# Loading the rows of the first two loop blocks at the end of attention, in a fused attention and mixture-of-experts kernel

## The chip, the cores and the metric

The kernel runs on one core of one Trainium2 chip. The metric is the device time of one execution in microseconds. The median of three runs of the kernel before is 657.54 us (655.55 to 658.39).

A core has five engines that run side by side and wait for one another by semaphores: TensorE (PE in the profile; PEld is its loading of weights), VectorE (DVE), ScalarE (ACT), GpSimd (POOL) and SyncE (SP), which here issues most of the DMAs. Each takes its own instructions in program order, so an instruction that waits holds up all that are queued behind it on its engine.

## The reference

Attention with keys and values averaged over groups of 8 rows, then a mixture of 8 experts in which each token goes to the one expert with the highest logit:

```python
k_p, v_p = (x.reshape(B, H, Sp, 8, D).mean(axis=3) for x in (k, v))
attn = softmax(q @ k_p.T / sqrt(D))
x = (attn @ v_p).transpose(0, 2, 1, 3).reshape(4608, 512)
expert_idx = argmax(x @ w_gate)                   # 8 experts
y = maximum(x[of e] @ w1[e], 0) @ w2[e]           # w1: 512x1024, w2: 1024x512
out = gate_w[:, None] * y                         # gate_w: softmax weight of the chosen expert
```

B = 8 batches, H = 8 heads, S = 576 rows, D = 64. The inputs are drawn with a fixed seed.

## The kernel before

**Attention** runs as 36 units of 128 tokens (line 912). A unit's tokens get their logits, and groups of four units (at the end, of two) are routed by `route(gidx)`: VectorE finds each token's expert, TensorE counts ranks, and GpSimd scatters each token's row, with its number and its gate, into `xs`, a table in HBM in which every expert has its own segment. `cum` holds the running counts; `c16` is its copy for TensorE. Small steps of this routing are kept in a list (`later`) and put in between the attention's own instructions (`fill`, `drain`), and scatters go through a list of their own (`flush`). Hooks (`put(unit, place, function)`) set other work at places in the units: loads, and splits of weights.

All products of the experts are made of 16-bit halves: a 32-bit number is split into a high half (ScalarE) and the rest (VectorE), and three matmuls replace one. This holds for weights (`wsplit`) and for rows (`split_x`).

**A block** is up to 256 rows of one expert. `up(s, f, n)` makes 128 of the 1024 hidden columns, with 12 matmuls; `relu_hi` (ScalarE) and `relu_lo` (VectorE) split the result; `finish(s, j, half)` makes the output for 128 of the rows from half of the hidden columns, with 12 matmuls. Both need the rows with the columns on the partitions: `turn` or `trans` transposes the halves of the rows by DMA from SyncE, and after `trans`, which goes by way of `xTs`, `arrive` (VectorE) copies them into `xT`.

**Block 0** is the first 256 rows of expert 0. When 256 tokens of expert 0 have been counted early enough, `early_load` (unit 29) brings its rows into `xg`, GpSimd splits them, `turn` transposes them, and the first three `up` run in units 33 to 35. Then `okf` is 1 and the table starts at block 1.

**The hand-over** (lines 972 to 1173): the other five `up` of block 0 run while VectorE ends the routing (`counted`, `ordered`, `ended`) and works out a table (`table`, 29 small steps) of which rows each loop block takes and which experts' weights come next. `tables` transposes it on TensorE into `tabs`. Only then come block 0's four `finish`, and the loads of blocks t=0 and t=1, whose places are read from `tabs`. Their rows are split, t=0's are transposed, the next expert's weights are loaded whole (`wwhole`, two DMAs of 2 MB), then t=2's rows are loaded, and t=1's rows are transposed.

**The loop** (line 1208) takes one block a turn. In turn t SyncE transposes the rows of t+2 and loads those of t+3, and in turns where an expert begins (and in t=0) ScalarE and VectorE split the next expert's weights (`part`) behind the split of rows:

```python
        arrive()
        split_x()
        part(s, en)
        if full:
            for half in range(2):
                finish(s, 1, half)
        take(1)
```

`take` reads the outputs from PSUM, `give` scatters them from GpSimd; `keep_ids`, `move_ids` and `take_ids` pass rows' numbers and gates along on GpSimd and mark `xg` as free. PSUM tiles named `pq` share two buffers, taken in turn.

Of the kernel before, what the change touches and what calls it, by code (L numbers as in the profile page):

```python
# [11 lines left out]
I32 = mybir.dt.int32  # L12
# [19 lines left out]
def kernel(  # L32
# [147 lines left out]
    for x in range(2):  # L180
# [17 lines left out]
    oki = consts.tile([1, 1], I32, name="oki")  # L198
    gC, gA, gB = (consts.tile([128, 2], F32, name=n) for n in ("gC", "gA", "gB"))
# [22 lines left out]
    xg, xg2 = (VB[i].rearrange("p y c s x -> p (y c s x)").bitcast(F32)[:, 0:2 * XW]  # L222
               .rearrange("p (j x) -> p j x", j=2) for i in (2, 0))
# [361 lines left out]
    EARLY = len(bounds) - 4  # L585

    def route(gidx):
# [39 lines left out]
        def rank():  # L627
            oh = Z["oh"][:, 0:gs]
            pm = psA.tile([128, 512], F32, name="pq", bufs=2)
            pr = pm[:, 0:gs * E].rearrange("p (u e) -> p u e", e=E)  # L630
            nc.tensor.matmul(pr, before, oh, start=True, stop=False, skip_group_check=True)
            nc.tensor.matmul(pr, ones, Z["c16"][:, None, :].to_broadcast([128, gs, E]), start=False, stop=False,
                             skip_group_check=True)
            for u in range(1, gs):
                nc.tensor.matmul(pr[:, u:gs, :], ones, oh[:, 0:gs - u, :], start=False, stop=False,
                                 skip_group_check=True)
            Z["pr"] = pr

# [48 lines left out]

        if gidx == len(bounds) - 1:
            return [top, away, best, lowest, before_all, onehot, count, carry], rank, \
                [ranked, spot, spot_int, total, ident_ids, guard, gate], soft, scatters  # L690
        chain = [top, away, best, lowest, before_all, onehot, soft, rank, count, ranked, carry, total, spot, spot_int,
                 ident_ids, guard, gate, scatters]
        if gidx == EARLY - 1:
            chain += [before_all, early_pe, early_int, early_shift, lambda: (flush(), KVS.update(early=1))]
        for f in chain:
            later(gidx, f, f in (rank, early_pe))
# [161 lines left out]

    put(28, "sp", blank_x, xg)
# [9 lines left out]
    put(31, "sp", turn)  # L869

# [134 lines left out]

    def sent(st):
        for o in scat + soon:
            tc.declare_no_dep(st.ins, o.ins, reason="rows of other tokens")
        scat.append(st)
        return st  # L1010
# [17 lines left out]
    def ended():  # L1028
        pe = psA.tile([128, 512], F32, name="pq", bufs=2)
        pq["nb"] = pe[:, 0:E]  # L1030
        nc.tensor.matmul(pq["nb"], ones, pq["lt"], start=True, stop=True)
        for f in back:
            f()
        scatters()
        flush()
        pad_rest()
        table()

    def table():
        nb, pos, more = pq["nb"], pq["pos"], pq["more"]  # L1040
        tcl, ex_, sb, blk, nw = (tf[:, NK + j:NK + j + 1] for j in range(5))
        g = work.tile([128, 2, E], F32, name="gg")
        end = work.tile([128, E], F32, name="end")
        n3 = work.tile([128, 3], F32, name="n3")
        sel = work.tile([128, 4, E], F32, name="sel", bufs=1)
        exk, got, par = (work.tile([128, n], F32, name=m) for n, m in ((4, "exk"), (4, "got"), (4, "par")))
        tot = work.tile([128, 1], F32, name="tot")
# [3 lines left out]
        V.tensor_reduce(tot, end, axis=AX.X, op=OP.max)  # L1051
        V.tensor_scalar(tcl, tot, -1.0, tv, op0=OP.add, op1=OP.min)
# [29 lines left out]
    def tables():  # L1082
        pt = psA.tile([128, 512], F32, name="pq", bufs=2)
        nc.tensor.transpose(pt[0:NK, 0:128], tf[:, 0:NK], ident)
        V.tensor_copy(tabs, pt[0:NK, 0:NT])

    for f in range(FC):
        if f >= len(UPAT):
            up(0, f, BLK)
        if f + 1 == 5:  # L1090
            counted()
            ordered()
        if f + 1 == 6:
            ended()
        if f + 1 == 8:
            tables()
        if f in (1, 3):
            relu_hi(f // 2)
    for k in (2, 3):
        relu_hi(k)  # L1100
    for k in range(4):
        relu_lo(k)
    views = [x.rearrange("p a b c -> p (a b c)") for x in qt] + [x.rearrange("p c x -> p (c x)")[:, 0:2048] for x in kv[1:]]
    views = [x.bitcast(F16) for x in views]
    W1[1] = [x.rearrange("p (c f) -> p c f", c=DC) for x in views[:2]]
    W2[1] = [x.rearrange("p (c f) -> p c f", c=FC) for x in views[2:]]
    pY.append(psA.tile([128, 512], F32, name="pq", bufs=2))
    pH[3] = psA.tile([128, 512], F32, name="pq", bufs=2)
    for j, half in ((1, 0), (1, 1), (0, 0), (0, 1)):
        finish(0, j, half)  # L1110
# [22 lines left out]
    xh2 = kv[1].rearrange("p c x -> p (c x)")[:, 0:1024].bitcast(F16).rearrange("p (j a x) -> p j a x", j=2, a=2)  # L1133
    blank_x(xg2)
    load_x(0)
    load_x(1, xg2)
    for j in range(2):
        x, h = xg[:, j, 0:Dm], xh[:, j]
        nc.scalar.activation(h[:, 0], x, AF.Copy)
        V.tensor_tensor(h[:, 1], x, h[:, 0], op=OP.subtract)  # L1140
    keep_ids()
    move_ids()
    turn()

    def at_place(j):
        return nc.values_load(tab[0:1, 1 + j:2 + j], engines=[ENG.SP], min_val=0, max_val=E - 1)

    wwhole(at_place(1), 0)
    load_x(2)
    split_x(xg2, xh2)  # L1150
    keep_ids(xg2)
    trans(xh2)
# [105 lines left out]
```

## Time and profile before

| | |
|---|---|
| median of three runs | 657.54 us (655.55 to 658.39) |
| the profiled execution's own time | 649.4 us |
| its span, first to last instruction | 647.3 us |
| mean granted clock of TensorE | 0.962 |
| TensorE busy | 584.5 us (90%) |
| VectorE, ScalarE, GpSimd busy | 349.6, 289.1, 258.2 us |

The span is the time from the first to the last instruction of the profiled execution, 2.1 us below the time of that execution. Times in the timeline are microseconds from the start of the span. A busy TensorE is not one at its peak, as matmuls overlap in the pipeline. The loop's first `up` starts at 240.78, and the loop takes the rest of the span.

### The profile page before, as it was taken

The page shows a single profiled execution, that of the slowest core. Times are in us where ns is not written, and L with a number is a line of the kernel's source. Part 1 is how long each engine was busy: PE and PEld are TensorE (multiplying, and loading weights), DVE is VectorE, ACT ScalarE, POOL GpSimd, SP SyncE. Part 2 cuts the span into 40 slices and gives each one's busy share as a digit, 9 for nine tenths or more (in the row PEclk, how much of TensorE's full clock was granted, in tenths as well). Part 3 has the DMA queues.
Part 4 walks back from the last instruction along what each step waited for, and adds up shares of the span by engine and source line. Part 5 has one row for each costly group of instructions (what it writes and reads, how often), then busy time and mean ns, then how long its engine had stood idle before and what let it go on. Part 6 is the DMA issues. An engine that isn't in the chain of part 4 may idle for free. (4 is left out here: it accounts for less than half of the span.)

```text
span 647.3 us, 15827 instructions
## 1 busy us (share of the span) xinstructions
PE 584.5 (90%) x4630; PEld 430.7 (67%) x4631; DVE 349.6 (54%) x767; ACT 289.1 (45%) x634; POOL 258.2 (40%) x475
## 2 busy tenths in 40 slices
PE   6669979878878779899999999999999999999985
PEld 4558878778867537566776677676667677667653
DVE  5669969899898821712362221237122641273783
ACT  1447858658864121621452222236223622263772
POOL 5793576887466621330232012223113032214134
PEclk9979989779999988999999999999999999999988
DMA  8971797957734459497377213335723392329200
GB/s 252 320 226 56 226 311 177 294 157 239 200 107 102 171 144 338 118 379 218 99 225 229 54 39 85 97 79 164 250 59 94 68 327 75 92 43 331 41 30 10
DMA packets 104170, 105.59 MB, mean 163 GB/s; under 512 B 62278, under 2 KB 72518, under 8 KB 104136
## 3 DMA queue, kind: packets, MB, share of 16 engines
q1 hardware_dynamic: 97496, 85.46, 46.9%
q0 software_dynamic: 6640, 19.71, 8.4%
q8 instruction: 18, 0.29, 0.2%
q14 instruction: 16, 0.13, 0.1%
HBM read 71.77 MB, written 22.06 MB: 145 GB/s over the span
## 5 line engine op out<-in xcount | busy, mean ns | idle before, releaser
L964 PEld LDWEIGHTS <-bd 128*128 128x128 f16 x936 | 91.8, 98 | 106.9 <-issue 2.1
L958 DVE SCALAR_TENSOR_TENSOR bd<-ps,bd 128x512 f16<-128x512 f32 x44 | 30.1, 690 | 154.2 <-ACT bd L954 154.1
L1167 POOL TENSOR_TENSOR spacer<-ql,iG 1x1 f32<-1x1 f32 x44 | 22.7, 516 | 188.3 <-ACT ql L1163 187.3
L495 ACT ACTIVATE both<-ps,nmx 128x72 f32<-128x72 f32 x288 | 68.7, 326 | 34.1 <-DVE nmx L488 33.5
L478 PE MATMUL ps<-bd,qT 128*128 128x144 f32 x256 | 50.4, 326 | 11.0 <-ACT both L495 5.8
L964 PE MATMUL po<-kv,bd 128*128 128x512 f16 x264 | 58.8, 379 | 0.0
L964 PE MATMUL po<-w,bd 128*128 128x512 f16 x264 | 58.8, 379 | 0.0
L954 ACT ACTIVATE bd<-ps 128x512 f16<-128x512 f32 x44 | 26.1, 596 | 72.9 <-PE L900 58.3
L1168 POOL DMA_INDIRECT out_dram<-ql,iG x44 | 44.7, 1017 | 21.2 <-issue 20.1
L318 POOL TENSOR_TENSOR st<-kv 128x1280 f32<-128x1280 f32 x14 | 40.8, 2913 | 25.8 <-DMA kv<-in_k_dram 23.3
L660 POOL DMA_INDIRECT x_by_expert<-both,rpos x36 | 35.2, 979 | 37.6 <-DVE ri L566 16.1
L902 PE MATMUL ps<-kv,qt 128*128 128x256 f16 (+1 forms) x176 | 46.7, 270 | 2.7 <-DVE qt L113 2.6
L900 PE MATMUL ps<-kv,w 128*128 128x256 f16 (+1 forms) x176 | 44.3, 265 | 5.1 <-DMA kv<-bd 3.4
L478 PEld LDWEIGHTS ps<-bd,qT 128*128 128x128 f32 x256 | 40.1, 215 | 12.8 <-ACT both L495 9.7
L964 PE MATMUL pq<-kv,bd 128*128 128x512 f16 x216 | 48.1, 379 | 0.0
L901 PE MATMUL ps<-kv,qt 128*128 128x256 f16 (+1 forms) x176 | 46.8, 270 | 0.0
L900 PE MATMUL ps<-kv,qt 128*128 128x256 f16 (+1 forms) x176 | 46.7, 270 | 0.1
L902 PE MATMUL ps<-kv,w 128*128 128x256 f16 (+1 forms) x176 | 44.3, 265 | 0.7 <-DVE qt L113 0.6
L964 PE MATMUL pq<-w,bd 128*128 128x512 f16 x192 | 44.4, 389 | 0.0
L901 PE MATMUL ps<-kv,w 128*128 128x256 f16 (+1 forms) x176 | 44.3, 265 | 0.0
L900 PEld LDWEIGHTS <-w 128*128 128x128 f16 x352 | 34.8, 99 | 10.2 <-issue 3.9
L902 PEld LDWEIGHTS <-qt 128*128 128x128 f16 x352 | 35.2, 100 | 7.2 <-issue 3.7
(246 smaller groups left out, 1364.8 us busy)
## 6 DMA issues: line engine op xcount, KB each, us to landing
st<-in_moe_w_dram SPq DMA_DIRECT2D x8, 2048.0 KB, 13.4
both<-in_moe_w_dram SPq DMA_DIRECT2D x6, 2048.0 KB, 12.9
vb<-x_by_expert SPq DMA_DIRECT2D x17, 514.0 KB
kv<-in_k_dram SPq DMA_DIRECT2D x7, 1024.0 KB
kv<-in_v_dram SPq DMA_DIRECT2D x7, 1024.0 KB
qt<-in_q_dram SPq DMA_DIRECT2D x6, 1024.0 KB
st<-in_moe_w_dram SPq DMA_DIRECT2D x4, 1024.0 KB
qt<-in_q_dram SPq DMA_DIRECT2D x4, 512.0 KB
```

The costliest lines, as they stand in the source:

```text
L318: nc.gpsimd.tensor_tensor(t1, src[:, :, 0:4 * D], src[:, :, 4 * D:], op=OP.add)
L478: nc.tensor.matmul(ps[:, x * 2 * KP:(x + 1) * 2 * KP], t[:, h, :], BD[b % 3][:, :, h, :], start=True, stop=True)
L495: nc.scalar.activation(p[:, h * KP:(h + 1) * KP], ps[:, x * KP:(x + 1) * KP], AF.Exp, bias=nmx[:, x:x + 1], scale=-1.0)
L660: st = nc.gpsimd.indirect_dma_start(out=xs, out_offset=bass.IndirectOffsetOnAxis(ap=Z["pos"][:, u:u + 1], axis=0), in_=X[:, u, :], in_offs ...
L900: nc.tensor.matmul(dst, wh, xT[:, d, 0:n], start=(d == 0), stop=False)
L901: nc.tensor.matmul(dst, wh, xT[:, DC + d, 0:n], start=False, stop=False)
L902: nc.tensor.matmul(dst, wl, xT[:, d, 0:n], start=False, stop=(d == DC - 1))
L954: nc.scalar.activation(hT[0][:, 2 * k:2 * k + 2, :].rearrange("p f t -> p (f t)"), pH[k], AF.Relu)
L958: V.scalar_tensor_tensor(l, pH[k], 0.0, h, op0=OP.max, op1=OP.subtract)
L964: nc.tensor.matmul(y, hT[x][:, f, 128 * j:128 * j + 128], W2[s][z][:, f, :], start=(half == x == z == f == 0), stop=(half == z == 1 and f ...
L1167: nc.gpsimd.tensor_tensor(spacer[:, 0:1], ys[j][0:1, 0:1], iG[0:1, j:j + 1].bitcast(F32), op=OP.add)
L1168: st = nc.gpsimd.indirect_dma_start(out=out, out_offset=bass.IndirectOffsetOnAxis(ap=iG[:, j:j + 1], axis=0), in_=ys[j], in_offset=None, b ...
```

## The change

- A flag `okf2` is set when, with group 7 (units 28 to 31) about to be counted, expert 0 already has 768 tokens and block 0 was loaded early.
- If it is set, `load_again` in unit 35 loads the rows of blocks 1 and 2 of expert 0, which are then t=0 and t=1. It needs the scatters of groups 0 to 6. `xg2` moves from a buffer that attention uses to its end to one that is free by then, and its blanking (`blank_x`) to unit 32.
- The rows of t=0 are split and transposed while block 0's `up` run, those of t=1 are split behind the table. If the flag is not set, both are loaded and split behind the table as before.
- t=0's rows go by `trans` and `arrive` and no longer by `turn`. The transposition of t=1's rows comes ahead of the weights' load.
- The steps of the hand-over are put in another order: `counted` and `ordered` one `up` later, `ended` as well; `relu_lo` of the first half ahead of `ended`; the table's work behind `relu_lo`; and `tables` behind three of the four `finish`.

```diff
+    xh2 = kv[1].rearrange("p c x -> p (c x)")[:, 0:1024].bitcast(F16).rearrange("p (j a x) -> p j a x", j=2, a=2)
...
+    AGAIN = EARLY + 1
...
+            if gidx == AGAIN:
+                nc.tensor.matmul(pm[:, 256:257], ones, Z["c16"][:, 0:1], start=True, stop=True, skip_group_check=True)
+                Z["pa"] = pm[:, 256:257]
...
+        def again():
+            V.tensor_scalar(okf2, Z["pa"], 768.0, okf, op0=OP.is_ge, op1=OP.mult)
+
+        def again_int():
+            V.tensor_copy(oki2, okf2[0:1, :])
...
+        if gidx == AGAIN:
+            x = chain.index(ranked) + 1
+            chain[x:x] = [again, again_int, lambda: (flush(99, AGAIN - 1), KVS.update(again=1))]
...
+    def load_again():
+        assert KVS.pop("again")
+        ok = nc.values_load(oki2[0:1, 0:1], engines=[ENG.SP], min_val=0, max_val=1)
+        with tc.If(ok > 0):
+            lds = [nc.sync.dma_start(x, xs[b * BLK:b * BLK + BLK, :].rearrange("(j p) x -> p j x", p=128))
+                   for b, x in ((1, xg), (2, xg2))]
+        for ld in lds:
+            for o in scat[bounds[AGAIN][0]:]:
+                tc.declare_no_dep(ld.ins, o.ins, reason="rows of other tokens")
+            soon.append(ld)
+
+    put(32, "q", blank_x, xg2)
...
+    put(35, "sp", load_again)
...
-        table()
+        ends()
...
-        if f + 1 == 5:
+        if f + 1 == 6:
             counted()
             ordered()
-        if f + 1 == 6:
+            split_x()
+            trans()
+            relu_lo(0)
+            relu_lo(1)
+        if f + 1 == 7:
             ended()
-        if f + 1 == 8:
-            tables()
         if f in (1, 3):
             relu_hi(f // 2)
     for k in (2, 3):
         relu_hi(k)
-    for k in range(4):
+    for k in (2, 3):
         relu_lo(k)
+    table()
+    split_x(xg2, xh2)
...
+    pt = psA.tile([128, 512], F32, name="pq", bufs=2)
     pY.append(psA.tile([128, 512], F32, name="pq", bufs=2))
+    finish(0, 0, 0)
+    finish(0, 1, 0)
+    finish(0, 1, 1)
+    tables(pt)
     pH[3] = psA.tile([128, 512], F32, name="pq", bufs=2)
-    for j, half in ((1, 0), (1, 1), (0, 0), (0, 1)):
-        finish(0, j, half)
+    finish(0, 0, 1)
...
-    blank_x(xg2)
-    load_x(0)
-    load_x(1, xg2)
-    for j in range(2):
-        x, h = xg[:, j, 0:Dm], xh[:, j]
-        nc.scalar.activation(h[:, 0], x, AF.Copy)
-        V.tensor_tensor(h[:, 1], x, h[:, 0], op=OP.subtract)
+    ok = nc.values_load(oki2[0:1, 0:1], engines=[ENG.SP, ENG.Activation, ENG.DVE], min_val=0, max_val=1)
+    with tc.If(ok < 1):
+        load_x(0)
+        load_x(1, xg2)
+        split_x()
+        trans()
+        split_x(xg2, xh2)
+    arrive()
     keep_ids()
     move_ids()
-    turn()
...
+    keep_ids(xg2)
+    trans(xh2)
     wwhole(at_place(1), 0)
     load_x(2)
-    split_x(xg2, xh2)
-    keep_ids(xg2)
-    trans(xh2)
```

`ends` is the first four lines of the old `table`, up to the total of blocks.

## Rows read from the trace of the kernel before

**Rows 1.** Timeline of TensorE, first `up` of blocks t=2 and t=3: start, us, instruction.
```profile
288.00 0.27 PE L900 MATMUL ps<-kv,w 128*128 128x256 f16 x1
...
308.84 0.27 PE L900 MATMUL ps<-kv,qt 128*128 128x256 f16 x1
```

**Rows 2.** Timeline of TensorE, hand-over and t=0; in brackets idle time before, and releaser.
```profile
217.15 0.17 PE L984 MATMUL pq<-c,ones 128*128 128x8 f16 x1 [0.84 <-DVE c L977]
...
225.06 0.27 PE L1084 MATMUL pq<-ident,tf 128*8 128x128 f32 x1 [3.70 <-DVE tab L1080]
...
240.78 0.37 PE L900 MATMUL ps<-kv,w 128*128 128x256 f16 x1 [3.40 <-DMA kv<-bd]
...
259.08 5.34 PE L964 MATMUL po<-w,bd 128*128 128x512 f16 x24
...
266.11 0.27 PE L900 MATMUL ps<-kv,w 128*128 128x256 f16 x1 [1.69 <-ACT qt L111]
```

**Rows 3.** 1 us stretches: PE, PEld, DVE, ACT, POOL busy; PEclk, DMA, GB/s.
```profile
245.00:246.00 1.00, 1.00 (x6) 0.73 (x5) 0.00 (x0) 0.00 (x0) 0.54 (x4) 0.50 1.03 303
...
255.00:256.00 1.00, 1.00 (x6) 0.47 (x5) 0.66 (x1) 0.00 (x0) 0.00 (x0) 1.00 1.08 363
256.00:257.00 1.00, 1.00 (x7) 0.47 (x5) 0.00 (x0) 0.00 (x0) 0.00 (x0) 1.00 2.13 107
```

**Rows 4.** Timeline of VectorE in block t=0.
```profile
259.47 0.69 DVE L847 COPY kv<-kv 128x2048 f16<-128x2048 f16 x1 [3.81 <-DMA kv<-kv]
...
262.53 1.22 DVE L836 TENSOR_TENSOR bd<-vb,bd 128x1024 f16<-128x1024 f32 x1 [2.36 <-ACT bd L835]
263.67 4.62 DVE L113 SCALAR_TENSOR_TENSOR qt<-st,qt 128x1024 f16<-128x1024 f32 x4
```

**Rows 5.** Timeline of GpSimd, hand-over and t=0.
```profile
205.40 0.97 POOL L660 DMA_INDIRECT x_by_expert<-both,rpos  x1 [0.22 <-issue]
...
226.96 0.98 POOL L226 MEMSET vb<- 128x1028 f32 x1
...
234.73 0.19 POOL L815 TENSOR_TENSOR gC<-vb,zf 128x2 f32<-128x2 f32 x1 [6.63 <-DMA vb<-x_by_expert]
...
259.75 0.47 POOL L815 TENSOR_TENSOR gC<-vb,zf 128x2 f32<-128x2 f32 x1 [14.20 <-SPq L1208]
```

**Rows 6.** Timeline of the SyncE queue, hand-over and t=0.
```profile
230.78 2.76 SPq L1122 DMA_DIRECT2D vb<-x_by_expert  x2
...
236.17 2.64 SPq L840 DMA_TRANSPOSE kv<-bd  x2
240.09 0.96 SPq L86 DMA_DIRECT2D st<-in_moe_w_dram  x2
...
246.18 11.28 SPq L843 DMA_TRANSPOSE kv<-kv  x1
263.92 1.98 SPq L843 DMA_TRANSPOSE kv<-bd  x1
```

**Rows 7.** Costliest groups of the page: weight loads of `finish`.
```profile
L964 PEld LDWEIGHTS <-bd 128*128 128x128 f16 x936 | 91.8, 98 | 106.9 <-issue 2.1
```

**Rows 8.** Timeline of VectorE, routing's tail, table and relu_lo.
```profile
217.35 0.17 DVE L987 TENSOR_TENSOR lt<-pq,thr 128x8 f16<-128x8 f32 x1 [0.26 <-PE pq L984]
...
219.60 0.15 DVE L640 TENSOR_TENSOR rt<-pq,roh 128x16 f32<-128x16 f32 x1
...
221.43 0.21 DVE L1052 TENSOR_SCALAR tf<-tot,tv 128x1 f32<-128x1 f32 x1
...
225.49 1.27 DVE L958 SCALAR_TENSOR_TENSOR bd<-ps,bd 128x512 f16<-128x512 f32 x2
...
226.69 1.27 DVE L958 SCALAR_TENSOR_TENSOR bd<-pp,bd 128x512 f16<-128x512 f32 x2
```

**Rows 9.** Instructions of lines 1153 and 1203: durations in ns, least, median, most.
```profile
L1153 DVEq TENSOR_LOAD <-tab x1: 994/994/994, 238.6 to 238.6; - x1
...
L1203 PEldq COMPARE_BRANCH  x61: 71/186/3661, 235.9 to 621.6; - x61
```

More of the change, by code (lines that the diff above doesn't have):

```diff
@@ L198 @@
     oki = consts.tile([1, 1], I32, name="oki")
+    okf2 = consts.tile([128, 1], F32, name="okf2")
+    oki2 = consts.tile([1, 1], I32, name="oki2")
     gC, gA, gB = (consts.tile([128, 2], F32, name=n) for n in ("gC", "gA", "gB"))
@@ L221 @@
     ys = [x.rearrange("p h d -> p (h d)") for x in ql]
-    xg, xg2 = (VB[i].rearrange("p y c s x -> p (y c s x)").bitcast(F32)[:, 0:2 * XW]
-               .rearrange("p (j x) -> p j x", j=2) for i in (2, 0))
+    xg, xg2 = (x[:, 0:2 * XW].rearrange("p (j x) -> p j x", j=2) for x in (
+        VB[2].rearrange("p y c s x -> p (y c s x)").bitcast(F32), kv[2].rearrange("p c x -> p (c x)")))
+    xh2 = kv[1].rearrange("p c x -> p (c x)")[:, 0:1024].bitcast(F16).rearrange("p (j a x) -> p j a x", j=2, a=2)
     def blank_x(x):
@@ L1004, with at_place @@
     n0, n1 = 2, 0
+    def at_place(j):
+        return nc.values_load(tab[0:1, 1 + j:2 + j], engines=[ENG.SP], min_val=0, max_val=E - 1)
     def sent(st):
@@ L1036, in ended, with ends @@
         pad_rest()
-        table()
[L1039 to L1047, printed above, removed]
+        ends()
+    def ends():
+        nb, more = pq["nb"], pq["more"]
+        end = pq["end"] = work.tile([128, E], F32, name="end")
+        tot = pq["tot"] = work.tile([128, 1], F32, name="tot")
         V.tensor_tensor(more, more, nb[:, None, :].to_broadcast([128, E, E]), op=OP.mult)
@@ L1051, in table @@
         V.tensor_reduce(tot, end, axis=AX.X, op=OP.max)
+    def table():
+        pos, end, tot = pq["pos"], pq["end"], pq["tot"]
+        tcl, ex_, sb, blk, nw = (tf[:, NK + j:NK + j + 1] for j in range(5))
+        g = work.tile([128, 2, E], F32, name="gg")
+        n3 = work.tile([128, 3], F32, name="n3")
+        sel = work.tile([128, 4, E], F32, name="sel", bufs=1)
+        exk, got, par = (work.tile([128, n], F32, name=m) for n, m in ((4, "exk"), (4, "got"), (4, "par")))
         V.tensor_scalar(tcl, tot, -1.0, tv, op0=OP.add, op1=OP.min)
@@ L1080, in table, with tables @@
         V.tensor_tensor(tab[0:1, 0:1], tot[0:1], okf[0:1, :], op=OP.subtract)
-    def tables():
-        pt = psA.tile([128, 512], F32, name="pq", bufs=2)
+    def tables(pt):
         nc.tensor.transpose(pt[0:NK, 0:128], tf[:, 0:NK], ident)
@@ L1131, in load_x @@
                     part(128, 64, x[0:64, 1])
-    xh2 = kv[1].rearrange("p c x -> p (c x)")[:, 0:1024].bitcast(F16).rearrange("p (j a x) -> p j a x", j=2, a=2)
-    blank_x(xg2)
-    load_x(0)
-    load_x(1, xg2)
-    for j in range(2):
-        x, h = xg[:, j, 0:Dm], xh[:, j]
-        nc.scalar.activation(h[:, 0], x, AF.Copy)
-        V.tensor_tensor(h[:, 1], x, h[:, 0], op=OP.subtract)
+    ok = nc.values_load(oki2[0:1, 0:1], engines=[ENG.SP, ENG.Activation, ENG.DVE], min_val=0, max_val=1)
[6 more added lines that the diff above has]
+    arrive()
     keep_ids()
     move_ids()
-    turn()
-    def at_place(j):
-        return nc.values_load(tab[0:1, 1 + j:2 + j], engines=[ENG.SP], min_val=0, max_val=E - 1)
+    keep_ids(xg2)
+    trans(xh2)
     wwhole(at_place(1), 0)
     load_x(2)
-    split_x(xg2, xh2)
-    keep_ids(xg2)
-    trans(xh2)
     with tc.If(nc.values_load(tab[0:1, 1:2], engines=[ENG.Activation, ENG.DVE, ENG.SP], min_val=0, max_val=1) > 0):
```

## The prediction

> **What bounds the kernel now.** I read the views in this order: the page, for who is busy; TensorE's timeline through the hand-over from attention to the expert loop, for its idle places; the same stretch on VectorE, the SyncE queue and GpSimd, for what ends each place; and the stretches of 1 us for clock and DMA. The chain that ended last says little here: it stops at the last outputs. TensorE is the bound in the loop: two successive blocks start 20.84 us apart with no idle time between them [rows 1], so what can be won lies in front of the loop and in its first turns. The reader should see four idle places there [rows 2]: 0.84 us before the count matmul (c16 not yet cast); 3.70 us before the transposition of the table, while VectorE works the table out; 3.40 us before the loop's first `up`, which waits for the DMA transposition of block 1's rows; and, when block t=0 has ended at 259.08+5.34 = 264.42, a stall before t=1. Block t=1 would have started at 288.00-20.84 = 267.16 had it run without gaps [rows 1, 2], so this stall is worth 2.74 us. The third place also costs clock: it is followed by a granted clock of 0.5, the 1.2 GHz level, until 246 [rows 3], and t=0 takes 264.42-240.78 = 23.64 us, 2.80 more than a later block. The 1.69 us wait at 266.11 was followed by no such fall.
>
> Why t=1 stalls matters most. In t=0 VectorE splits the next expert's weights, after block t=2's rows (x2) have come and been split, and TensorE's `up` in t=1 waits for the first half of that split. Call S the start of VectorE's first weight split: S = 263.67 [rows 4], and t=1 effectively starts at S+3.49. S follows from GpSimd's 259.75 by 3.92 us. GpSimd had waited for SyncE to enter the loop [rows 5], and SyncE sat 11.28 us in issuing the transposition of xg2's halves, queued behind 4 MB of weights [rows 6]. The weights were issued at 240.09; DMA traffic falls from 363 to 107 GB/s at 256 [rows 3, 6], so weights and x2 together had landed 15.9 us after the issue.
>
> **The change, part by part.** *Does it act?* Worked out from the reference's inputs, expert 0 gets 1018 tokens, all in attention units 0 to 27; the test wants 768 by then. Those counts also give 17 full and 5 half blocks, 39 halves of 24 weight loads, which is the 936 of [rows 7]. So the new branch is taken as written: no load and no split behind the table.
>
> *Rows come early.* Group 6's last scatter is issued at 205.40+0.97 [rows 5]; `blank_x`, moved ahead of it on GpSimd, takes 0.98 plus a small memset, so 207.5. A row load took 234.73-230.78 = 3.95 us from issue to use [rows 5, 6]. With that for the scatter too, the loads issue at 211.5 and xg is there by 215.5, xg2 half a us later. VectorE wants xg, split by ScalarE, at 219.9 (below): more than 3 us of cover, and every us past that costs one. Two small VectorE operations and one matmul are added in attention, 0.2 us each, beside waits on TensorE: nothing, at most 0.5. The memset may hold VectorE up by 0 to 0.98; I take 0, since the two splits that ran beside it before, from 226.69, took 1.27 as the two ahead of it did [rows 5, 8].
>
> *TensorE* runs `up` f=3 to 7 with no wait for c16 and ends near 220.2 instead of 221.4; half of block 0's `finish` no longer waits for the table. That takes away the 0.84 and nearly all of the 3.70. VectorE orders it now: the count's first operation moves from 217.35 to about 217.65, one `up` column later but without the wait.
>
> *VectorE's chain* [rows 4, 8]: counted and ordered 2.25 (217.35 to 219.60), to 219.9; xg's split 1.14 (262.53 to 263.67), to 221.0; relu_lo 0 and 1, 1.27, to 222.3; routing's tail and `ends` 1.83 (219.60 to 221.43), to 224.1; relu_lo 2 and 3, 1.27, to 225.4; table 3.6 (221.43 until TensorE's wait for it ends at 225.06), to 229.0; xg2's split 1.14, to 230.1; table cast, load of the flag and branch 1.0 (0.99 for such a load, [rows 9]), to 231.1; `arrive` 0.69, to 231.8. xg's transposition was issued at 221.1 and is long there. TensorE meanwhile waits about 0.9 us for `ends` (a PSUM buffer is still read) and for the table, ends block 0 at about 232, and t=0 starts at 232.2 instead of 240.78, at full clock: it ends at 253.0 instead of 264.42, 11.4 us earlier.
>
> *What is late next: S.* SyncE's queue is now: transposition of xg2's halves after `arrive` (1.98 us at the steady price [rows 6], no weights ahead of it), to 233.8; then 1.28 us (236.17+2.64 to 240.09) to the weights' issue, 235.1 instead of 240.09; then x2. Queued behind `arrive` are thus both weight loads and x2, and GpSimd, ScalarE and VectorE wait for these. SyncE enters the loop early, so landing decides: 235.1+15.9 = 251.0; GpSimd 0.3 later; S = 251.3+3.92 = 255.2; t=1 starts effectively at 258.7. Against 267.16 that is 8.5 us earlier: some 3 us of what t=0 gained is given back in a longer stall (253.0 to 258.7). TensorE idles over 4 us in one piece there, longer than the 3.40 that brought the low clock, so I add 0 to 2.80 and take 1.2, as half of the slow stretch would lie under the wait for the split. GpSimd's last scatters and pads move 2.7 us later with VectorE's chain; the load of before that waited for the pads went out at 230.78, so 233.5, ahead of x2.
>
> Sum: 0.84, 3.70, 3.40 and 2.80 are gone, 0.9 and 3.0 come back, the clock takes 1.2, and the rest is overlap: 267.16-258.7-1.2 = 7.3 us. Span 647.3 to 640.0, the profiled execution 649.4 to 642.1. The runs shown have their median at 657.54, 8.1 above the profiled execution; I carry the saving over in us: **650.3 us**.
>
> Its own range: if weights and x2 flow 3 us faster (4.2 MB of weights, 512x1024 and 1024x512 floats, and 0.5 MB of x2 take 13 us at the 363 GB/s of [rows 3]) and the clock holds, 11.5 us are won, 646.0; if VectorE's chain is 2 us longer and the full 2.80 is paid, 3.7, so 653.8.
>
> **The rivals.**
> (a) *S is no bound*: x2 comes by 246 or t=1's wait is shorter, and TensorE runs straight on: 267.16-253.0 = 14.2 us at most, 643.3; between, 645. For it: 15.9 us includes a slow start of the stream. Against: 4.7 MB at the rate of [rows 3] can't land before 248.
> (b) *A jump costs a code fetch.* One branch on TensorE took 3.66 us, the median of that line is 0.19 [rows 9]. If VectorE's new skip ahead of `arrive` costs that, everything behind shifts: 653.9. Against: the last such skip there, L1153, was followed by nothing late; SyncE's and ScalarE's new skips lie under waits.
> The Trainium skill, "Runtime: NRT & Kernel Launch", Instruction fetch mechanics, says that a taken branch to a target outside the fetched pages stalls for the fetch; by it (b) would come about at any skip to a far target, with 653.9. One branch among the 61 on TensorE agrees; no run here shows how far VectorE's skip reaches.
> (c) *Rows late*: if the load waits for group 7's scatters too, xg comes near 222, VectorE sits in front of everything behind its split for 3.3 us: 653.6.
> (d) *Hidden anyway*: the weights stream, not the hand-over, sets S, and slowed by the scatters of outputs beside it S moves by under 5 us while the clock falls: 656.
> (e) *Slower: the flag is 0.* Then the loads wait for table and pads (233.5 instead of 230.78, 2.7 us), both splits and two transpositions follow one another ahead of the weights (the second 1.98), so t=1 comes about 4 us later: 661.5. It decides below 768 counted tokens; [rows 7] speak against it.
>
> **How the numbers follow.** Forecast 0.62; (a) 0.13; (b) 0.08; (c) 0.05; (d) 0.06; (e) 0.06. About 0.5%, 3.3 us, is what a measurement of this kernel can tell from no change. Faster: the first four less 0.04 for their upper ends, 0.84; same: (d) and those 0.04, 0.10; slower 0.06. The range leaves out (d), (e) and the outer half of (a): 645.0 to 654.2.
>
> **What would show it.** No idle over 1.5 us on TensorE from the count matmul to t=0; t=0's `up` near 232 at full clock; VectorE's table ending near 229; weights issued near 235 and ahead of them a transposition issued in about 2 us; S near 255; a longer stall before t=1, with a fall of the clock. Wrong if xg's split makes VectorE wait, if the weights are issued past 237, or if S follows something other than x2's landing.

## The result

| | before | after |
|---|---|---|
| median of 20 executions each | 655.87 us (650.93 to 660.85) | 648.80 us (642.88 to 655.19) |
| the profiled execution's span | 647.3 us | 645.6 us |
| mean granted clock of TensorE | 0.962 | 0.943 |
| ratio of the times | | 0.989, 95% interval 0.9863 to 0.9918 |

The kernel is faster by 1.1%, 7.1 us between the medians. Forecast were 7.3 us and 650.3, from a base of 657.54 (655.87 over the twenty executions). The profiled executions of order_old and turn_behind, below, are over 1.5% longer than the fastest of their kernels, and only their stretch behind unit 35, as defined here, is read. The two profiled spans differ by only 1.7 us, and the first reading has to clear that up. The rows are unit 35's normalisation in VectorE's timeline (start and duration in us, engine, line, operation), first of before, then of after:

```profile
214.02 0.69 DVE L568 TENSOR_TENSOR both<-po,ri 128x512 f32<-128x512 f32 x1
```
```profile
217.67 0.69 DVE L571 TENSOR_TENSOR both<-po,ri 128x512 f32<-128x512 f32 x1
```

The attention of this one execution of after took 3.65 us longer, and nearly all of that was there ahead of the first changed instruction. In the traces of the experiments the same place comes anywhere from 213.5 to 230.9. So I compare what lies **behind unit 35**: from this row to the end before took 647.29-214.02 = 433.27 us and after 427.91. Second traces of both kernels (below) took 434.75 and 427.98. This stretch repeats to 0.1 us in the two traces of after and to 1.5 us in the two of before, and the mean difference is 6.1 us. Times of after that are set against the prediction have 3.65 taken off.

TensorE of after, timeline of the hand-over and the first blocks, with the idle time and what ended it in brackets; these answer to [rows 1, 2]:

```profile
232.62 0.27 PE L1119 MATMUL pq<-ident,tf 128*8 128x128 f32 x1 [0.64 <-DVE tf L1115]
...
235.90 0.27 PE L930 MATMUL ps<-kv,w 128*128 128x256 f16 x1 [0.42 <-DVEq L1245]
...
259.20 0.28 PE L930 MATMUL ps<-kv,w 128*128 128x256 f16 x1 [2.30 <-ACT qt L111]
261.04 0.40 PE L932 MATMUL ps<-kv,w 128*128 128x256 f16 x1 [1.45 <-DVE qt L113]
262.18 0.39 PE L932 MATMUL ps<-kv,w 128*128 128x256 f16 x1 [0.31 <-DVE qt L113]
...
285.73 0.27 PE L930 MATMUL ps<-kv,w 128*128 128x256 f16 x1
```

The places of 0.84, 3.70 and 3.40 us are gone; 0.64 and 0.42 are left. t=0 starts at 235.90. Ahead of and in t=1 there are now 2.30 us and 1.45+0.31+0.32+0.31 = 2.39 us. VectorE, SyncE and GpSimd, answering to [rows 4 to 6, 8]:

```profile
221.37 0.17 DVE L1017 TENSOR_TENSOR lt<-pq,thr 128x8 f16<-128x8 f32 x1 [0.62 <-PE pq L639]
...
223.72 1.23 DVE L852 TENSOR_TENSOR bd<-vb,bd 128x1024 f16<-128x1024 f32 x1
...
234.12 0.69 DVE L863 COPY kv<-kv 128x2048 f16<-128x2048 f16 x1 [0.21 <-DVEq L1177]
...
259.77 4.62 DVE L113 SCALAR_TENSOR_TENSOR qt<-st,qt 128x1024 f16<-128x1024 f32 x4
```
```profile
234.91 2.01 SPq L859 DMA_TRANSPOSE kv<-kv  x1
238.46 1.09 SPq L86 DMA_DIRECT2D st<-in_moe_w_dram  x2
241.42 3.51 SPq L1165 DMA_DIRECT2D vb<-x_by_expert  x1
```
```profile
255.96 0.19 POOL L831 TENSOR_TENSOR gC<-vb,zf 128x2 f32<-128x2 f32 x1 [14.77 <-DMA vb<-x_by_expert]
```

The split of t=0's rows (223.72) has no wait in front of it. SyncE no longer sits in the transposition (2.01 us in place of 11.28), the weights go out at 238.46, and GpSimd, the first to use x2, now waits for its landing and no longer for SyncE. Clock and DMA in stretches of 1 us (columns as in [rows 3]):

```profile
252.00:253.00 1.00, 1.00 (x6) 0.48 (x5) 0.00 (x0) 0.00 (x0) 0.00 (x0) 1.00 1.05 392
254.00:255.00 1.00, 1.00 (x6) 0.42 (x5) 0.00 (x0) 0.00 (x0) 0.00 (x0) 1.00 0.32 109
...
261.00:262.00 1.00, 0.82 (x3) 0.34 (x3) 1.00 (x1) 1.00 (x3) 0.04 (x1) 0.50 0.80 152
...
268.00:269.00 1.00, 1.00 (x11) 0.89 (x10) 1.00 (x2) 0.21 (x1) 0.96 (x2) 1.00 0.50 146
```

The stream ends near 255. At 261, with 2.30 and 1.45 us of waiting over, the clock falls to 1.2 GHz, until 268.

### The profile page after: what moved, and what is told of

Its sections match the earlier page's. It is cut to its first block, busy times and chain, and to the rows that moved or that the text cites. A ratio compares the mean times of both kernels' runs of the same rounds, so it can differ in the third digit from the quotient of the medians.

```text
span 645.6 us, 15876 instructions
## 1 busy us (share of the span) xinstructions
PE 583.1 (90%) x4631; PEld 429.8 (67%) x4632; DVE 355.4 (55%) x769; ACT 289.0 (45%) x633; POOL 261.3 (40%) x475
## 5 line engine op out<-in xcount | busy, mean ns | idle before, releaser
L539 PE MATMUL po<-vb,ph 128*128 128x146 f16 (+2 forms) x384 | 32.4, 232 | 12.5 <-DVE l L574 7.1
L994 PE MATMUL pq<-w,bd 128*128 128x512 f16 x192 | 42.7, 379 | 0.0
```

The costliest lines, as they stand in the source:

```text
L539: nc.tensor.matmul(po[:, half, cols], a[:, c * 128:(c + 1) * 128], VB[b % 3][:, y, c, sl, 0:CW], start=st, stop=False, skip_group_check=True)
L994: nc.tensor.matmul(y, hT[x][:, f, 128 * j:128 * j + 128], W2[s][z][:, f, :], start=(half == x == z == f == 0), stop=(half == z == 1 and f ...
```

## The experiments

Each is an edit of after unless it says otherwise. "Behind unit 35" is the stretch defined above: before 433.27 and 434.75, after 427.91 and 427.98.

| kernel | ratio to before, 95% interval | behind unit 35, us |
|---|---|---|
| after_again | 0.988 (0.9835 to 0.9926) | 427.98 |
| before_again | 0.9985 (0.9932 to 1.0037) | 434.75 |
| x2_first | 0.9901 (0.9866 to 0.9936) | 428.3 |
| weights_early | 0.9939 (0.9905 to 0.9973) | 431.9 |
| turn_behind | 0.9852 (0.9817 to 0.9888) | 426.3 |
| flag_zero | 1.0100 (1.0066 to 1.0134) | 440.3 |
| half_first | 0.9871 (0.9831 to 0.9911) | 421.0 |
| filler | 0.9876 (0.9831 to 0.9921) | 427.5 |
| rows_late | 0.9972 (0.9933 to 1.0010) | 432.0 |
| order_old | 0.9943 (0.9901 to 0.9985) | 431.8 |
| split_first | 0.9928 (0.9894 to 0.9962) | 426.3 |
| x2_filler | 0.9924 (0.9893 to 0.9955) | 426.7 |

**Both kernels once more.** after_again is after, before_again is before, unchanged.

> The kernel after, unchanged, to have it on the same chip beside split_first and x2_filler. Theory: 0.989, and in its trace again an idle place of 2 to 5 us ahead of t=1 that ends with the first piece of the split. A second trace also tells whether the fall of the clock there comes each time, and whether the attention ahead of unit 35 again takes another time than in the first (theory: it does, by some us in either direction, and the change has no part in it).

> The kernel before, unchanged, for a second trace of it. From unit 35's normalisation to the end, the two traces of after take 427.91 and 427.98 us and the first of before 433.27, a difference of 5.3, while the times of many executions differ by 7.1 to 7.6. Theory: before varies behind unit 35 and its first trace was one of the shorter ones (its wait of 1.69 us ahead of t=1 brought no fall of the clock, waits of over 2 us in after did): the second trace takes 434.5 to 436 there, with a slow stretch ahead of or in t=1. Rival: the second trace takes 433.3 again, and the missing 2 us lie in the attention, where the added steps change the pattern of slow stretches. Ratio in time 1.000 within its interval.

After repeats itself: 427.98, with 2.06 us ahead of t=1 and a slow stretch there again. Before took 434.75, in the range of the first theory, and its waits fell out otherwise. TensorE of before_again:

```profile
235.36 0.27 PE L1084 MATMUL pq<-ident,tf 128*8 128x128 f32 x1 [1.96 <-DVE n L1076]
250.78 0.27 PE L900 MATMUL ps<-kv,w 128*128 128x256 f16 x1 [3.10 <-DMA kv<-bd]
273.23 0.28 PE L900 MATMUL ps<-kv,w 128*128 128x256 f16 x1 [1.44 <-ACT qt L111]
```

The 3.10 us ahead of t=0 brought no fall of the clock here (t=0 took 273.23-250.78 = 22.45 us and not 25.33), the fall came in t=1 instead. So the 2.80 us that the prediction booked for the 3.40 us place is not fixed to that place. One us of the 7.1 stays without a place behind unit 35. It is less than the interval of the ratio leaves open (1.8 us either way), and two traces of each kernel can't locate it; whether the change costs or gains anything in attention is not shown.

**The parts of the change: order_old, rows_late, flag_zero.**

```diff
 order_old: early loads, steps of the hand-over in before's order
+ f+1 == 5: counted(), ordered();  f+1 == 6: ended(), table();  f+1 == 8: tables(pt)
+ then relu_lo(0..3), split_x(), trans(), split_x(xg2, xh2), all four finish
 rows_late: the early loads also wait for group 7's scatters
-            for o in scat[bounds[AGAIN][0]:]:
+            for o in scat[bounds[AGAIN + 1][0]:]:
 flag_zero: the flag never comes true
-            V.tensor_scalar(okf2, Z["pa"], 768.0, okf, ...
+            V.tensor_scalar(okf2, Z["pa"], 65536.0, okf, ...
```

> Early loads alone: the rows of t=0 and t=1 come as in the kernel after, but the steps of the hand-over stand in the order of before (counted and ordered behind the fifth up, the table right behind the routing's tail and ahead of the relu_lo, the table's transposition ahead of all four finish). Theory by the prediction's terms: the idle places of 0.84 and 3.70 us stay, the 3.40 us ahead of t=0 and its 2.80 us of slow clock go; the copy of t=0's rows comes near 233.5 on the clock of before, the weights go out near 237.5 in place of 240.09, and t=1 starts some 3 to 4 us earlier than before: ratio 0.994 (0.9925 to 0.995). Rival (the order of steps adds nothing, as the weights' stream sets t=1): 0.989. Other rival (the loads alone are worth nothing without the order): 0.998 or more.

> The kernel after, with the early loads also waiting for group 7's scatters. Theory (VectorE has 3 us of cover ahead of the split of t=0's rows, and what passes it delays all that is behind): group 7's last scatter is issued at 217.95 in the trace of after and lands near 221.5, the rows come 4 us later, VectorE waits 2 to 3 us for them, table, copy and weights' issue move by that: ratio 0.992 to 0.994. Rival (the wait ahead of t=1 or other slack takes it in): 0.989.

> The changed kernel with a threshold of 65536 instead of 768, so that the flag is 0 and the rows of t=0 and t=1 are loaded and split behind the table; the early split and transposition of xg still run, on what lies in the buffer, and are overwritten. Prices the rival of the prediction: t=0 starts about 5 us later than in the kernel before, t=1 about 4 us later; ratio to the kernel before 1.006. If the new order of the steps carried the gain without the early rows, the ratio would stay at 0.99.

order_old gave 0.9943, as expected: early loads alone are worth about half of the change in time (0.6 of 1.1%, with 0.4% either way) and a third behind unit 35 (2.2 of 6.1 us). The rest comes when the new order of the steps is added; that order without the early rows is a loss (flag_zero, below). Its TensorE waits again for c16 and for the table:

```profile
225.87 0.17 PE L1014 MATMUL pq<-c,ones 128*128 128x8 f16 x1 [0.81 <-DVE c L1007]
234.24 0.37 PE L1119 MATMUL pq<-ident,tf 128*8 128x128 f32 x1 [4.15 <-DVE tab L1116]
```

rows_late lost 4.1 us behind unit 35, more than the 3.3 of rival (c). Its time, 0.8% or 5.4 us longer than after's with some 3 us either way, is above the expected 0.992 to 0.994. VectorE and TensorE:

```profile
231.12 1.22 DVE L852 TENSOR_TENSOR bd<-vb,bd 128x1024 f16<-128x1024 f32 x1 [4.13 <-ACT bd L851]
```
```profile
233.00 1.89 PE L994 MATMUL po<-w,bd 128*128 128x512 f16 x4 [3.90 <-DVE bd L988]
```

The loads go out 4.05 us behind unit 35's row, in after 3.40 us ahead of it, as the last scatter has to land first. VectorE stands 4.13 us in front of the split: of 7.45 us 3.3 were covered, as the prediction had it ("more than 3"). But behind VectorE TensorE's `finish` waits too (3.90 us), the granted clock falls to 1.2 GHz in this wait, and the next 24 products take 7.08 us, at full clock 5.34. So the table's transposition gets its turn later still, and the copy of t=0's rows comes 5.5 us late and not 4.1. "Every us past that costs one" was too cheap.

flag_zero is rival (e): 1.010, 6.6 us of 655, more than the expected 1.006. TensorE stands 12.82 us ahead of t=0, since rows, split and transposition follow the table one after another:

```profile
261.85 0.37 PE L930 MATMUL ps<-kv,w 128*128 128x256 f16 x1 [12.82 <-DVEq L1245]
```

The new order without the early rows is thus slower than before; the flag decides about 2% of the time.

**Does the hand-over or the split set t=1? filler.**

```diff
+    for _ in range(28):
+        nc.tensor.matmul(pH[3][:, 0:BLK], hT[0][:, 0, 0:128], W2[0][0][:, 0, 0:BLK], start=True, stop=True)
```

> The kernel after, with 28 matmuls of 256 columns (0.109 us each, 3.05 us) that nothing needs put on TensorE between block 0's last product and t=0. Theory (t=1 is set by the split of the weights, and t=0 ends too early for it): the 3.05 us vanish in the wait ahead of t=1, and the ratio stays at 0.988 to 0.990, or falls to 0.986 if the shorter wait spares the fall of the clock (1.4 us or so). Rival (the hand-over on TensorE sets the time): 3.05 us more, 0.9935.

With the useless work t=0 starts 22.75 us behind unit 35's row, in after 18.23: 3.05 us of matmuls and 1.5 us more waiting. It cost nothing: 0.9876, and 427.5 behind unit 35, 0.4 less than after. TensorE's start of t=1:

```profile
259.51 0.27 PE L930 MATMUL ps<-kv,w 128*128 128x256 f16 x1 [2.28 <-DVE qt L113]
```

This is the last wait of that block. The four inside t=1 are gone (2.39 us in after), and no stretch of the loop's first blocks has a low clock (3.3 us in after, worked out below): the two pay for the 4.5 us. The 2.28 us are no wait for the split, though the row names it. TensorE's queue was through its branch at the end of t=0 by 256.42, and then one load of a register took 1.43 us, with a median of 0.31 (durations in ns: least, median, most):

```profile
L1159 PEldq TENSOR_LOAD <-tabs x21: 303/313/1430, 234.9 to 613.2; - x21
```

In after TensorE thus comes to t=1 too early, and the four waits inside t=1, each ended by VectorE's split, are what it gains by that. The prediction's step that S, and no longer the hand-over, sets t=1 is shown by these waits, by their absence here, and by half_first below; both figures, 2.39 us of waits and 3.3 of clock, are of one trace, and the clock's part is the larger.

**What S waits for: x2_first, weights_early, turn_behind.**

```diff
 x2_first
+    load_x(2)
     wwhole(at_place(1), 0)
-    load_x(2)
 weights_early: in the loop over f
             trans()
+            wwhole(at_place(1), 0)
 turn_behind
-    keep_ids(xg2)
-    trans(xh2)
     wwhole(at_place(1), 0)
     load_x(2)
+    keep_ids(xg2)
+    trans(xh2)
```

> The changed kernel with the load of t=2's rows (x2) issued ahead of the two weight loads instead of behind them; nothing else differs. Theory (t=1 waits for the split that starts at S, and S waits for x2, queued behind 4 MB of weights): x2 lands near 243 instead of 256, its split follows block t=0's relu directly, S falls from 259.8 to about 252 on the clock of the changed kernel's profile, TensorE runs from t=0 into t=1 without the idle time of 2.3 and 1.45 us and without the fall of its clock; block t=2 starts 8 us earlier. Time 8 us below the changed kernel: ratio to the kernel before 0.977. Rival (the weights' own landing holds the split): the weights land 1.5 us later, S moves later by as much, ratio 0.990 to 0.992.

> The changed kernel with the two weight loads issued right behind the transposition of t=0's rows, ahead of everything that waits for the table; the transposition of t=1's rows and the load of x2 now stand behind them in SyncE's queue. Theory (S follows the weights' issue, as x2 stands behind them): issue near 230 instead of 238.5, x2 landed by 246, S near 250, no idle time between t=0 and t=1, 8 us below the changed kernel, ratio 0.977. Rival (the transposition of t=1's rows, now held behind the weights, comes too late for t=1): TensorE waits at t=1 for the transposed rows, up to 4 us, ratio 0.983 or more.

> The changed kernel with the transposition of t=1's rows put back behind the weights and x2, the order of the kernel before; the weights then no longer wait for VectorE's arrive. Theory: weights issued near 231, SyncE held in issuing the transposition until they are through, so it enters the loop near 250 and S is set by that again, near 255 instead of 259.8; t=1 starts effectively 6 us earlier than in the changed kernel, ratio 0.980. Rival (the transposition ahead of the weights is what the change gains by): S later than 259.8, ratio 0.992 or more.

x2_first moved S from 42.1 to 36.5 us behind unit 35's row (some 8 us were foretold), and the ratio, 0.9901, shows no gain over after. ScalarE now waited for the first 2 MB of weights, issued at 244.17, and TensorE stood longer ahead of t=1 than in after:

```profile
255.07 3.90 ACT L111 ACTIVATE qt<-st 128x1024 f16<-128x1024 f32 x4 [3.17 <-DMA st<-in_moe_w_dram]
```
```profile
266.79 0.37 PE L930 MATMUL ps<-kv,w 128*128 128x256 f16 x1 [6.40 <-DVE kv L113]
```

The rival (weights' landing) has its 3.17 us, but it is not what held TensorE: the pieces that `up` needs were ready by 261, t=0 had ended at 260.4, and the releaser named in the row writes the other half of the weights, which t=1's `up` doesn't read. That question led to x2_filler, below.

In weights_early the weights went out at 239.42, behind the transposition of t=0's rows, and TensorE stood 7.49 us ahead of t=0:

```profile
235.63 2.43 SPq L859 DMA_TRANSPOSE kv<-bd  x1
239.42 1.09 SPq L86 DMA_DIRECT2D st<-in_moe_w_dram  x2
```
```profile
255.65 0.37 PE L930 MATMUL ps<-kv,w 128*128 128x256 f16 x1 [7.49 <-DVEq L1245]
```

The copy of the rows came at 254.2, 18.6 us after the transposition's issue; in order_old it comes 4.4 us after. But the transposition was not late: its 2048 packets of 256 bytes ran from 236.8 to 239.6, ahead of the weights' first packet at 240.6. What was late is SyncE. It stood at the branch around the late loads of t=0's and t=1's rows (line 1178 in this kernel) from 243.8 to 254.1, until the first 2 MB of weights had landed (the last mark of their landing is at 254.08), and VectorE's copy waited for SyncE at this branch. SyncE's wait (us in total, times, longest), then VectorE's copy:

```profile
SPq L1178 <- SPq L1178: 10.3, 1, 10.3
```
```profile
254.21 0.69 DVE L863 COPY kv<-kv 128x2048 f16<-128x2048 f16 x1 [8.40 <-SPq L1178]
```

In after the weights go out behind that branch. Sending 4 MB early is no gain here, since SyncE comes through the next branch, for which VectorE waits, only when the first 2 MB are there. Neither expectation had this wait.

turn_behind sent the weights 7.1 us earlier than after, relative to unit 35, but x2 then waited for the last scatters and pads, which had to pass beside the weights, and SyncE sat 8.19 us in the transposition of t=1's rows, so that GpSimd came late to x2. A row of its waits (us in total, times, longest), then SyncE and GpSimd:

```profile
SPq L1165 <- DMA x_by_expert<-zpad,padi: 6.3, 2, 5.3
```

```profile
244.59 2.86 SPq L86 DMA_DIRECT2D st<-in_moe_w_dram  x2
256.24 0.37 SPq L1165 DMA_DIRECT2D vb<-x_by_expert  x1
257.14 8.19 SPq L859 DMA_TRANSPOSE kv<-kv  x1
```
```profile
267.64 0.46 POOL L831 TENSOR_TENSOR gC<-vb,zf 128x2 f32<-128x2 f32 x1 [11.71 <-SPq L1245]
```

With 0.9852 (0.9817 to 0.9888) it is between the two expectations and meets neither; S comes 1.3 us earlier than in after. No loss against after is shown, and behind unit 35 it is 1.6 us shorter: that the change puts the transposition of t=1's rows ahead of the weights has no gain in these runs.

**Taking S away from x2: half_first, split_first.**

```diff
 half_first: in a block of the loop (part takes the pieces' numbers)
         arrive()
+        part(s, en, range(4))
         split_x()
-        part(s, en)
+        part(s, en, range(4, 8))
 split_first: in a block of the loop
         arrive()
+        part(s, en)
         split_x()
-        part(s, en)
```

> The kernel after, but in a block of the loop the first half of the next weights' split (four pieces, w1) comes ahead of the split of the rows, and the second half behind it. Theory (the split waits only for x2, the rows of t=2, which land last; w1 has been there since about 249.3 in the trace of after, where the split begins at 259.77): the split begins right behind the copy of t=1's rows, near 251, the four pieces are ready before t=0 ends, t=1 follows t=0 with under 1 us of idle time and no fall of the clock. That is 264.9-257.7 = 7.2 us less than after: ratio to before 0.977 to 0.979. Rival 1 (another wait takes the place, as in x2_first, where TensorE was idle for 6.4 us though the pieces were there): 0.985 to 0.989. Rival 2 (the rows' split, now 4.6 us later in each turn, makes the transposition of t+2 late): the gain is lost in the turns behind, 0.989 or more, with idle time ahead of t=2 or t=3.

> The kernel after, but in a block of the loop the whole split of the next weights comes ahead of the split of the rows, as one piece, so that no code is added. Theory: as in half_first the first pieces start right behind the copy of t=1's rows (near 251 on after's clock), t=1 follows t=0 with 1.3 us of idle time or less at full clock, some 7 us of span less than after; the 2.2 us that half_first lost outside of its span (4.1 to 4.5 us between span and device time in each of its executions, 2.1 in after) don't come, as the engines' programs have the length of after's. Ratio to before 0.980 to 0.984. Rival (half_first's profiled execution was a lucky one and the wait ahead of t=1 was worth little): 0.987 to 0.990, like after. Other rival (the rows' split, 9.2 us later in the turns that split weights, makes t+2 late): 0.990 or more, with idle time of TensorE ahead of t=2 or later blocks.

Behind unit 35 half_first did what was expected: the split starts at 250.57, t=1 follows with 1.28 us, the clock stays at 2.4 GHz, and 421.0 is 6.9 us less than after (7.2 expected).

```profile
250.57 4.63 DVE L113 SCALAR_TENSOR_TENSOR qt<-st,qt 128x1024 f16<-128x1024 f32 x4 [0.95 <-ACT qt L111]
```
```profile
257.40 0.27 PE L930 MATMUL ps<-kv,w 128*128 128x256 f16 x1 [1.28 <-ACT bd L851]
```

The time gives only 0.9871, no gain over after that these executions show, and the expected 0.977 to 0.979 lies outside of its interval. 2.2 us are lost outside of the span: device time less span is 4.1 to 4.5 us in all six executions, 1.8 to 2.5 in after's twenty. Two more fetches of code of 8 KB stand behind the last instruction in its trace than in after's; that they are the 2.2 us is not shown. The rest of what the trace promised I can't place: six executions with an interval 0.8% wide don't tell 0.987 from 0.983.

split_first adds no code, and the 2.2 us were gone (differences of 1.9 to 3.2). t=1 started well (1.59 us), but the last block waited for its weights' split. TensorE there and, on VectorE in the turn before, the weights' split with the rows' split behind it:

```profile
618.59 0.22 PE L930 MATMUL ps<-kv,qt 128*128 128x128 f16 x1 [2.60 <-ACT qt L111]
...
619.91 0.22 PE L932 MATMUL ps<-kv,qt 128*128 128x128 f16 x1 [1.05 <-DVE qt L113]
```
```profile
601.21 9.17 DVE L113 SCALAR_TENSOR_TENSOR w<-both,w 128x1024 f16<-128x1024 f32 x8 [2.48 <-ACT w L111]
610.30 1.22 DVE L852 TENSOR_TENSOR bd<-vb,bd 128x1024 f16<-128x1024 f32 x1
```

With the rows' split 9.2 us later, the transposition and the copy behind it come later too, and the turn before the last is a half block (10.54 us) with no slack for that: from its start to the last block's it took 15.36 us, in after 10.97. The second rival held, in the last turns and not where I looked for it. Behind unit 35 the trace is still 1.6 us shorter than after's, while the ratio, 0.9928, is no better than after's on the same chip (0.988); that difference stays open.

**What held TensorE in x2_first: x2_filler** (x2_first with the 28 matmuls of filler).

> x2_first with the 28 matmuls (3.05 us) of filler between block 0 and t=0. In x2_first TensorE was idle for 6.4 us ahead of t=1 though weights and rows were there; its queue had no record from 260.0 to 264.9, and in the first microseconds of that the DMA engines ran the transposition of t=2's rows (1047 packets of 256 bytes in one us) beside three fetches of code, one of which took 2.4 us. Theory (the turn of the loop fetches code, and this fetch stood behind the transposition's packets): with t=0 ending 3 us later, behind the transposition, the wait shrinks to under 2 us, and 3 us of added work make the kernel faster than x2_first by about 2 us: 0.986 to 0.988. Rival (the turn takes its 6 us whenever it comes): 3 us slower, 0.9945.

A row settles more than the times do. Branches of the loop on TensorE's queue (durations in ns: least, median, most), in x2_first, after_again and half_first:

```profile
L1240 PEldq COMPARE_BRANCH  x61: 71/186/8446, 239.0 to 623.7; - x61
```
```profile
L1240 PEldq COMPARE_BRANCH  x61: 71/186/3826, 233.2 to 617.3; - x61
```
```profile
L1241 PEldq COMPARE_BRANCH  x61: 71/186/3326, 234.7 to 611.2; - x61
```

One branch of 8.45 us, from 256.4 to 264.8, and 2.0 us of register work behind it lead to 266.79. In the same time the DMA engines ran the transposition of t=2's rows and three fetches of code (a stretch of 1 us, and the queues from 260 to 264):

```profile
261.00:262.00 1.00, 0.00 (x0) 0.00 (x0) 0.36 (x1) 1.00 (x2) 0.00 (x0) 1.00 2.77 116
```
```profile
q1 hardware_dynamic: 1560, 0.42, 108.2%
q14 instruction: 2, 0.02, 4.3%
q8 instruction: 1, 0.02, 2.6%
```

The DMA engines are filled by little data, 116 GB/s (their share can pass 1, as a packet's whole time counts where it starts). In all fourteen traces exactly one of TensorE's branches takes over 1.2 us, always the one at the end of t=0, where the loop's end is reached for the first time: 3.2 to 4.2 us, and 8.45 in x2_first alone. Inside each of these branches lies one fetch of code of 16 KB (queue q8), and the branch ends 1.2 to 1.4 us after it, in x2_first 2.2. There the fetch starts only 4.6 us after the branch, in the other thirteen traces 1.0 to 1.8 us after it. Until 259.7 the second 2 MB of weights were still coming in, and from 257.6 the transposition's packets ran; which of the two held the fetch one execution doesn't tell. In x2_filler the branch took 4.0, TensorE's wait was 1.92 us, and with 3.05 us more work the kernel was 1.6 us shorter behind unit 35. The time, 0.9924 (0.9893 to 0.9955), misses the theory's 0.986 to 0.988 and leaves the rival's 0.9945 open; against x2_first's 0.9901 from another chip it confirms no gain. So only the trace speaks for the theory. The Trainium skill, "Runtime: NRT & Kernel Launch", Instruction fetch mechanics, has the rule that a taken branch out of the fetched pages waits for a fetch. This branch agrees; its price here is 3.2 to 4.2 us, or 8.45 in x2_first.

## Why the prediction was right

It forecast 7.3 us and 650.3; measured are 7.1 us and 648.8. Step by step, after's times less 3.65:

- *The flag and the rows.* The branch is taken as worked out. What the added steps in attention cost can't be seen beside attention's own differences of up to 10 us between traces. The cover of "more than 3 us" is 3.3 (rows_late).
- *TensorE's and VectorE's chains* were right to a few tenths. VectorE's first step 217.72 (forecast 217.65), the copy of t=0's rows 230.5 (231.1), t=0's start 232.25 (232.2), the weights' issue 234.8 (235.1).
- *The rest, called overlap.* The listed terms add up to 5.6 us, and the other 1.6 of the 7.3 stand in the sum as overlap without a row. The traces show what they are. In before the first half of block 0's `finish` ran mostly at the 1.2 GHz level (granted clock 0.5 from 226 to 229) and took 7.03 us, in before_again too; in after it takes 5.34. The 1.69 us are clock that the change gives back. First before, then after:

```profile
225.17 7.03 PE L964 MATMUL pq<-w,bd 128*128 128x512 f16 x24
```
```profile
226.64 5.34 PE L994 MATMUL pq<-w,bd 128*128 128x512 f16 x24
```

- *x2's landing* decides S, as forecast (GpSimd waits for just that transfer), and was 1.0 us late: use at 252.3, forecast 251.3. The 15.9 us from the weights' issue became 17.5; x2 goes out behind them (3.51 us in its issue) and comes after them. S is 256.1 (255.2).
- *The stall and the clock* were mis-sized, against each other. Forecast were 5.7 us of waiting and 1.2 for the clock. Measured: t=1 starts 259.20-235.90 = 23.30 us after t=0, 2.46 more than a full block, and t=2 another 26.53 after that, 5.69 more, of which 2.39 are the waits and 3.3 the clock. Waits 4.85, clock 3.3: the sum is 8.15 and not 6.9, and the first trace therefore shows t=2 5.9 us earlier than [rows 1], not 7.3. "Half of the slow stretch would lie under the wait" failed: the clock fell at 261, with most of the waiting over. That the median came out at 7.1 all the same is in part luck: before is longer in its second trace (434.75) than in the one that the forecast was read from, and one us has no place.
- *A row misread.* The 1.69 us ahead of t=1 in [rows 2], put down to the split, had another cause. The branch of 3.66 us of [rows 9] stood at 260.4 to 264.1 there, and 2.0 us of register work behind it lead to 266.11; ScalarE's first piece of the split (1.04 us), which the row names, was ready at 263.2. So 1.69 of the "stall worth 2.74 us" were no wait for the split. For the same reason the step "t=1 effectively starts at S+3.49" failed: the branch stood in that number. In after it is 285.73-20.84-3.3-259.77 = 1.8 us. In after the two waits end together: the branch takes 4.15 us and ends at 257.0, so that TensorE's queue is through near 259.0, and ScalarE's first piece is ready at 259.15; t=1 starts at 259.20. The 2.30 us are thus a wait for the split as much as for the branch; half_first, where the pieces are ready early, keeps 1.28 for the branch alone. ScalarE's split in before, then in after:

```profile
262.15 3.88 ACT L111 ACTIVATE qt<-st 128x1024 f16<-128x1024 f32 x4
```
```profile
258.11 3.88 ACT L111 ACTIVATE qt<-st 128x1024 f16<-128x1024 f32 x4
```

  Rival (b) had the right mechanism at the wrong engine: in after the skips on VectorE cost no more than the 0.21 us ahead of the copy, and the fetch is at TensorE's loop end, in both kernels alike.
- *The other rivals.* (a) falls: in after t=1 waits for the split. It is what half_first makes true in its trace, 421.0 behind unit 35. (c) was priced at 3.3 us and costs 4.1 behind unit 35, where the low clock comes on top. (d) falls, as S came 7.6 us earlier. (e) was priced at 4.0 us slower than before and costs 6.6; what the other 2.6 are wasn't taken apart.

## What to carry to other kernels

When an idle place is closed, look for the transfer that is now last: here half of the 11 us that t=0 gained was given back to the split behind a load that was queued behind 4 MB, and to the clock that fell there. What took that away, in a trace and not yet in the time, was to reorder the consumer (half_first), not the loads (x2_first, weights_early). Before putting a wait down to the releaser that a row names, look at the engine's own branches: in before a single one of 3.7 us explained a wait that looked like a missing operand. And before putting a late copy down to its transfer, look at the transfer's packets and at the branches between (weights_early). And where two executions differ more ahead of the change than the change is worth, compare from a fixed instruction near it to the end.

## What was not expected of the hardware

- The first passing of the loop's end costs TensorE's queue one branch of 3.2 to 4.2 us in thirteen traces, with one fetch of 16 KB inside it; in x2_first, where the fetch started late, 8.45 us.
- A DMA transposition of 0.5 MB was through 3.9 us after its issue though 4 MB of loads were issued 3.8 us behind it (weights_early). What came 18.6 us after its issue was its use, held by SyncE at a branch until the first 2 MB had landed.
- Device time less span grew from 2.1 to 4.3 us in the one kernel with more code on two engines (half_first), with two more code fetches behind the last instruction.
- Places with about the same wait were followed by a fall of the clock in one execution and not in the next: 3.40 us yes and 3.10 us no, 2.30 us with four short waits behind it yes, 2.28 us alone no.
